# An FFT and two MLPs on one core: the second MLP's matmuls read their moving operand from the last column down, and its weight tiles lie at other addresses

## The chip, the cores and the metric

One Trainium2 chip, one core of it. The metric is the device time of the kernel in microseconds (us). Engines: PE is TensorE (PEld its weight loads, LDWEIGHTS), DVE is VectorE, ACT is ScalarE, POOL is GpSimd, SP is SyncE, which issues the DMAs that the text speaks of. SBUF is the on-chip memory of 128 partitions that the engines read; PSUM is where TensorE writes.

## What is computed

The reference is a chain of three parts, all in fp32:

```python
X = np.fft.fft(np.fft.fft(x, axis=1), axis=2).real      # x: 4 x 3072 x 256
h = X.reshape(-1, 256) @ w_in                           # first MLP, 256 -> 2048 -> 256
x = np.maximum(0.01 * h, h) @ w_out
xp = x shifted by one token within its sequence         # second MLP
xk = mu_k * x + (1 - mu_k) * xp
xr = mu_r * x + (1 - mu_r) * xp
k = np.maximum(xk @ w_k, 0)                             # 256 -> 1024
v = (k * k) @ w_v                                       # 1024 -> 256
out = sigmoid(xr @ w_r) * v                             # gate, 256 -> 256
```

Matrix products are made of float32r matmuls. Each operand is split into a high part of fewer bits and a low part that holds the rest, and a product is three matmuls: high by high, low weight by high data, high weight by low data.

## The kernel before, in words

**First part.** The FFT is folded by its symmetries and its second axis is merged into the weights of the first MLP, so the first part of the span alternates between FFT matmuls (L303), and, for each of 4 sequences, 3 tiles of tokens and 16 slices of the hidden width, the matmuls of the first MLP (L569, L581, L592). At four places per sequence L613 multiplies weights of only 2 columns (`dc[b]["w"]`, one column and its low part) with 512 moving columns. L387 builds the merged weights at the start, from plain f32 operands. Each of these results goes to DRAM tiles `yd` as 128 partitions (features) by tokens.

**Second MLP.** There are 24 tiles of 512 tokens (`tiles`, W = 512). A tile x is 128 partitions x 2 (halves of the 256 features) x 512 tokens. All its matmuls have a weight slice of 128 x 128 as the stationary operand and 512 token columns as the moving one.

- `load_tile` (L740, L745) loads x and the shifted x; `prep` (L748) mixes them on ACT and DVE (L751, L752) and splits the result into `mh` and `ml` (L104, L111).
- `k_mm` (L902, matmul on L908): for each of 8 slices f of the hidden width, 6 matmuls (3 products x 2 feature halves) into one PSUM tile.
- `k_ev` (L911 to L913): ACT takes the maximum with 0, DVE multiplies it with the PSUM tile to k squared, and `k_split` (L972) splits that into `k2h` and `k2l`.
- `v_mm` (L943, matmul on L951): for each slice f, 6 matmuls (3 products x 2 output halves) that add to two PSUM tiles over all 8 slices.
- `r_mm` (L953, matmul on L959): for each output half, 6 matmuls, then the sigmoid on ACT (L961) into `sig`.
- `finish` (L963): DVE multiplies `sig` with the sum of `v_mm` (L966), and SP issues the store of the tile. The last tile is stored in two halves.

So a tile has 48 + 48 + 12 matmuls. Each matmul has its own weight load in front of it. The order is written out by hand: in each step f the loop issues `k_mm`, the evaluation, the split of the slice before, a gate half in two of the eight steps, and then `drain`, which runs `v_mm` for a slice that was split a step or more earlier. `early` does two slices of the first tile between the last steps of the first MLP.

**Where the operands lie.** `w2_alloc` (L689) makes the pool `w2p` on the right side of SBUF while the first MLP of the last sequence runs: `wkh`, `wkl` (128 x 2 x 1024), `wvh`, `wvl` (128 x 8 x 256) and `wrh`, `wrl` (128 x 2 x 256), all float32r, one behind the other. Each is a multiple of 512 bytes in each partition. The parts of the first five pieces of the weights are computed early, kept in DRAM and loaded there by DMA; the other pieces, the gate's among them, are written straight into these tiles by ACT (high part, L161) and DVE (low part, L166). The moving tiles `mh`, `ml`, `k2h`, `k2l` lie in the pool `p2`, behind a pad of 64 bytes.

Of the kernel before, what the change touches and what calls it, by code (L numbers as in the profile page):

```python
# [9 lines left out]
F32 = mybir.dt.float32  # L10
F32R = mybir.dt.float32r
U32 = mybir.dt.uint32
ACTF = mybir.ActivationFunctionType
ALU = mybir.AluOpType
# [3 lines left out]
P = 128  # L18
# [3 lines left out]
D = 256  # L22
FF = 2048
FK = 1024
NF = FF // P
NK = FK // P
# [52 lines left out]
def fft_mlp_kernel(ctx, tc, xs, x7, x8, x87, tb, tbs, alt, ce, so, mu, w_in, w_out, w_k, w_v, w_r, out):  # L79
    nc = tc.nc  # L80
    ctx.enter_context(tc.manual_schedule())
    V, A, T, G, Q = nc.vector, nc.scalar, nc.tensor, nc.gpsimd, nc.sync
# [16 lines left out]
    pqp = tc.alloc_tile_pool(name="pqp", bufs=1)  # L99
    work = tc.alloc_tile_pool(name="work", bufs=1)  # L100
    fft = tc.alloc_tile_pool(name="fft", bufs=1, side="right")

    def act_copy(o, i):
        A.activation(o, i, ACTF.Copy)  # L104
# [572 lines left out]
    w2 = {}  # L677
# [3 lines left out]
    for q in range(4):  # L681
        sl, s2 = slice(q * 256, (q + 1) * 256), slice(2 * q, 2 * q + 2)
# [6 lines left out]
    def w2_alloc():  # L689
        w2p = tc.alloc_tile_pool(name="w2p", bufs=1, side="right")  # L690
        w2["pool"] = w2p
        for nm, k, f in (("k", 2, FK), ("v", NK, D), ("r", 2, D)):
            for x in "hl":
                w2[nm + x] = w2p.tile([P, k, f], F32R, name=f"w{nm}{x}")
        w2["xp"] = tc.alloc_tile_pool(name="xp", bufs=1, side="right")
        for n in range(n_early):
            nm, _, at = sources[n]
            for x, k in zip("hl", kept[n]):
                Q.dma_start(at(w2[nm + x]).bitcast(F32), k)
# [104 lines left out]
    for b in range(B):  # L804
# [4 lines left out]
        for ti in range(NT):  # L809
# [3 lines left out]
            for u in range(NF):  # L813
                i = ti * NF + u
                x = nx
# [40 lines left out]
                if b == B - 1 and i == qe_u + 2:  # L856
                    fft.release()
                    w2_alloc()
# [43 lines left out]
    def k_mm(ps, f, xk):  # L902
        hi, lo = xk
        sl = slice(f * P, (f + 1) * P)
        i = 0
        for w, x in ((w2["kh"], hi), (w2["kl"], hi), (w2["kh"], lo)):
            for k in range(2):
                T.matmul(ps, w[:, k, sl], x[:, k], start=(i == 0), stop=(i == 5))  # L908
                i += 1

    def k_ev(ps, r, k2):  # L911
# [7 lines left out]
    for f in range(2):  # L919
        early.append([ps_s.tile([P, 512], F32, tag="s", name="ps"), small("h"), small("f")])  # L920
        k_mm(early[f][0], f, ready[0]["k"])
        if f == 0:
            step(None, None)
        k_ev(*early[f])
# [18 lines left out]
    def v_mm(f, kk, vps):  # L943
        hi, lo = kk
        ws = ((w2["vh"], hi), (w2["vl"], hi), (w2["vh"], lo))
        order = [(i, m) for i in range(3) for m in range(NB)]
        if f == NK - 1:
            order = [(i, m) for m in range(NB) for i in range(3)]
        for i, m in order:
            w, x = ws[i]  # L950
            T.matmul(vps[m], w[:, f, m * P:(m + 1) * P], x, start=(f == 0 and i == 0), stop=(f == NK - 1 and i == 2))  # L951

    def r_mm(xr, sig, m):  # L953
        hi, lo = xr
        ps = ps2.tile([P, 512], F32, tag="rps", bufs=2, name="rps")
        i = 0
        for w, x in ((w2["rh"], hi), (w2["rl"], hi), (w2["rh"], lo)):
            for k in range(2):
                T.matmul(ps, w[:, k, m * P:(m + 1) * P], x[:, k], start=(i == 0), stop=(i == 5))  # L959
                i += 1  # L960
        A.activation(sig[:, m], ps, ACTF.Sigmoid)  # L961

    def finish(ti, vps, sig):  # L963
        o = p2.tile([P, NB, W], F32, tag="o", name="o")
        for m in range(NB):
            V.tensor_tensor(o[:, m], sig[:, m], vps[m], op=ALU.mult)  # L966
            if ti == len(tiles) - 1:
                Q.dma_start(out[ti, :, m], o[:, m])
        if ti < len(tiles) - 1:
            Q.dma_start(out[ti], o)  # L970
# [7 lines left out]
    def drain():  # L978
        if q2:
            t, f, kk = q2.pop(0)  # L980
            if f == 0:
                t["v"] = [ps2.tile([P, 512], F32, tag="v", bufs=4, name=f"v{m}") for m in range(NB)]
            v_mm(f, kk, t["v"])
            if f == NK - 1:
                finish(t["i"], t["v"], t["sig"])

    def gate(t, m):
        r_mm(t["rk"], t["sig"], m)

    q1, q2 = [], []  # L990
    for ti in range(len(tiles)):
# [7 lines left out]
        for f in range(f0, NK):  # L999
            ps = ps2.tile([P, 512], F32, tag="k", bufs=2, name="kps")  # L1000
            r = p2.tile([P, W], F32, tag="r", bufs=3, name="rl")
            k2 = p2.tile([P, W], F32, tag="k2", bufs=3, name="k2")
            k_mm(ps, f, rd["k"])
            k_ev(ps, r, k2)
            if q1:
                tt, ff, kk2 = q1.pop(0)
                q2.append((tt, ff, k_split(kk2)))
            q1.append((t, f, k2))
            t["rk"] = rd.get("r")
            if not end and g0 <= f < g0 + NB:  # L1010
                gate(t, f - g0)
            if end and f == NK - 1:
                gate(t, 0)
            if len(q2) > 1:
                drain()
            if f == f0:
                for n in ((1, 2) if ti == 0 else (ti + 2,)):
                    if n < len(tiles):
                        loaded[n] = load_tile(n)
            if f == f1 and not end:  # L1020
                for g in todo:
                    g()
                todo = do_prep(ti + 1)
            if todo:
                todo.pop(0)()
# [83 lines left out]
```

## Time and profile before

| | |
|---|---|
| time, median of 2 runs | 1493.05 us (1492.74 to 1493.37) |
| the profiled execution, first to last instruction | 1490.7 us |
| TensorE busy | 1472.8 us, 6524 matmuls |
| VectorE busy | 1029.6 us |
| ScalarE busy | 893.1 us |
| GpSimd busy | 150.2 us |
| mean granted TensorE clock | 0.998 |

The span of the profiled execution is 2.3 us under the median of the timed runs; what lies around the first and the last instruction is not in it. A row of the groups reads: line, engine, operation, out<-in by the program's names, partitions x elements and type, how many | busy time in us, mean ns of one | idle time before. A row of the timeline reads: start in us from the start of the span, time in us, engine, line, operation, operands, how many were merged into the row. Matmuls are pipelined: one starts before the end of the one before it, so the distance between two starts is shorter than a duration. In rows that merge n instructions the time runs from the first start to the last end.

### The profile page before, as it was taken

The page shows a single profiled execution, that of the slowest core. Times are in us where ns is not written, and L with a number is a line of the kernel's source. Part 1 is how long each engine was busy: PE and PEld are TensorE (multiplying, and loading weights), DVE is VectorE, ACT ScalarE, POOL GpSimd, SP SyncE. Part 2 cuts the span into 40 slices and gives each one's busy share as a digit, 9 for nine tenths or more (in the row PEclk, how much of TensorE's full clock was granted, in tenths as well). Part 3 has the DMA queues.
Part 4 walks back from the last instruction along what each step waited for, and adds up shares of the span by engine and source line. Part 5 has one row for each costly group of instructions (what it writes and reads, how often), then busy time and mean ns, then how long its engine had stood idle before and what let it go on. Part 6 is the DMA issues. An engine that isn't in the chain of part 4 may idle for free.

```text
span 1490.7 us, 17784 instructions
## 1 busy us (share of the span) xinstructions
PE 1472.8 (99%) x6524; PEld 1212.0 (81%) x6524; DVE 1029.6 (69%) x1436; ACT 893.1 (60%) x1475; POOL 150.2 (10%) x162
## 2 busy tenths in 40 slices
PE   7999999999999999999999999999999999999998
PEld 4788888888888888888888887888888888888887
DVE  7897667766667766666767665676767666666675
ACT  4666566656566565665666666556565655555554
POOL 2444201132010222010000000000000000000000
PEclk9999999999999999999999999999999999999999
DMA  8657323464132654141320102221212112221200
GB/s 319 164 181 163 54 82 125 167 123 91 17 106 91 199 115 79 36 155 64 108 79 0 57 1 92 78 85 43 85 48 80 60 68 63 65 71 57 72 29 29
DMA packets 86258, 134.23 MB, mean 90 GB/s; under 512 B 29158, under 2 KB 49383, under 8 KB 82586
## 3 DMA queue, kind: packets, MB, share of 16 engines
q1 hardware_dynamic: 70906, 86.49, 18.0%
q0 software_dynamic: 15264, 46.60, 12.6%
q8 instruction: 51, 0.84, 0.2%
q14 instruction: 37, 0.30, 0.1%
HBM read 105.19 MB, written 27.88 MB: 89 GB/s over the span
## 4 chain that ended last, share of the span: by engine, by line
PE 96%; DVE 2%; ACT 1%; DMA 0%; issue 0%; ACTq 0%; DVEq 0%
PE o L592 35%; PE v L951 17%; PE kps L908 17%; PE ps L581 9%; PE ps L569 9%; PE rps L959 4%; PE wps L387 1%; PE dps L613 1%; PE cps L436 0%; DVE fv L139 0%; DMA st<-in_w_in 0%; PE wps L389 0%; PE f1Qe L303 0%; PE f2Qe L303 0%; DVE t0Pe L287 0%; PE f0Qe L303 0%
## 5 line engine op out<-in xcount | busy, mean ns | idle before, releaser
L658 DVE SCALAR_TENSOR_TENSOR g<-ev,ps 128x512 f32<-128x512 f32 x192 | 131.7, 686 | 184.2 <-PE ps L581 183.9
L912 ACT ACTIVATE rl<-kps 128x512 f32<-128x512 f32 x190 | 113.8, 599 | 230.7 <-PE kps L908 227.2
L640 DVE TENSOR_TENSOR gl<-g,gh 128x1024 fp32r<-128x1024 f32 x192 | 239.3, 1246 | 1.4 <-ACT gh L104 1.4
L913 DVE SCALAR_TENSOR_TENSOR k<-kps,rl 128x512 f32<-128x512 f32 x190 | 131.6, 692 | 148.6 <-ACT rl L912 147.8
L104 ACT ACTIVATE gh<-g 128x1024 fp32r<-128x1024 f32 x192 | 202.9, 1057 | 51.9 <-PE o L592 50.9
L592 PE MATMUL o<-gh,uoh 128*128 128x512 f32 x768 | 211.8, 390 | 0.0
L592 PE MATMUL o<-gh,uol 128*128 128x512 f32 x768 | 211.1, 389 | 0.0
L592 PE MATMUL o<-gl,uoh 128*128 128x512 f32 x768 | 211.1, 389 | 0.0
L107 ACT ACTIVATE g<-ps 128x512 f32<-128x512 f32 x192 | 114.8, 598 | 156.2 <-DVE g L658 155.0
L592 PEld LDWEIGHTS o<-gh,uoh 128*128 128x128 f32 x768 | 144.7, 188 | 30.6
L592 PEld LDWEIGHTS o<-gh,uol 128*128 128x128 f32 x768 | 144.2, 188 | 30.0
L592 PEld LDWEIGHTS o<-gl,uoh 128*128 128x128 f32 x768 | 144.2, 188 | 29.9
L574 DVE SCALAR_TENSOR_TENSOR ev<-cb,w,ps 128x512 f32<-128x512 f32 x192 | 143.3, 746 | 2.3 <-DVE g L658 0.5
L111 DVE TENSOR_TENSOR k2l<-k,k2h 128x512 fp32r<-128x512 f32 x190 | 129.6, 682 | 0.5 <-ACT k2h L104 0.5
L951 PE MATMUL v<-k2h,wvh 128*128 128x512 f32 x382 | 121.6, 389 | 0.1
L951 PE MATMUL v<-k2l,wvh 128*128 128x512 f32 x382 | 121.5, 389 | 0.0
L951 PE MATMUL v<-k2h,wvl 128*128 128x512 f32 x382 | 121.5, 389 | 0.0
L107 ACT ACTIVATE g<-g 128x512 f32<-128x512 f32 x192 | 119.9, 624 | 0.0
L908 PE MATMUL kps<-mh,wkh 128*128 128x512 f32 x380 | 117.3, 390 | 1.5 <-ACT mh L104 0.8
L104 ACT ACTIVATE k2h<-k 128x512 fp32r<-128x512 f32 x190 | 118.4, 623 | 0.0
L908 PE MATMUL kps<-ml,wkh 128*128 128x512 f32 x380 | 117.2, 390 | 0.1
L908 PE MATMUL kps<-mh,wkl 128*128 128x512 f32 x380 | 117.0, 389 | 0.0
(407 smaller groups left out, 2257.1 us busy)
## 6 DMA issues: line engine op xcount, KB each, us to landing
y<-yo SPq DMA_DIRECT2D x24, 512.0 KB
xa<-y SPq DMA_DIRECT2D x24, 512.0 KB
out_dram<-o SPq DMA_DIRECT2D x23, 512.0 KB
tab_a<-in_tbs POOLq DMA_DIRECT2D x8, 1158.0 KB, 6.2
tab_b<-in_tbs POOLq DMA_DIRECT2D x8, 1158.0 KB, 5.4
tab_c<-in_tbs POOLq DMA_DIRECT2D x6, 1158.0 KB, 5.4
tab_d<-in_tbs POOLq DMA_DIRECT2D x6, 1158.0 KB, 5.8
pm<-in_xs POOLq DMA_DIRECT2D x54, 128.0 KB, 3.4
```

The costliest lines, as they stand in the source:

```text
L104: A.activation(o, i, ACTF.Copy)
L107: A.activation(o, i, ACTF.Prelu, alpha=0.01)
L111: V.tensor_tensor(lo, src, hi.bitcast(F32), op=ALU.subtract)
L569: T.matmul(x["ps"], l[:, f], r, start=(i == 0), stop=(i == 2))
L574: V.scalar_tensor_tensor(x["ev"], x["cb"], w128[:, u:u + 1], x["ps"], op0=ALU.mult, op1=ALU.add)
L581: T.matmul(x["ps"], l[:, f], r, start=False, stop=(i == 2), skip_group_check=True)
L592: T.matmul(po[s][h], w[:, u % HF, h * P:(h + 1) * P], g[:, s], start=(u == 0 and i == 0), stop=(u == NF - 1 and i == 2))
L640: V.tensor_tensor(gl, x["g"], x["gh"].bitcast(F32), op=ALU.subtract)
L658: V.scalar_tensor_tensor(g[:, 1], x["ev"], 2.0, x["ps"], op0=ALU.mult, op1=ALU.subtract)
L908: T.matmul(ps, w[:, k, sl], x[:, k], start=(i == 0), stop=(i == 5))
L913: V.scalar_tensor_tensor(k2, ps, 0.0, r, op0=ALU.max, op1=ALU.mult)
L951: T.matmul(vps[m], w[:, f, m * P:(m + 1) * P], x, start=(f == 0 and i == 0), stop=(f == NK - 1 and i == 2))
```

## The change

All matmuls of the second MLP read their moving operand with a step of -1, from column 511 down to column 0. The product of `k_mm` therefore comes out with its tokens reversed, `v_mm` reverses it again, and the gate, which also comes out reversed, is read reversed in `finish`. The gate's high and low weights share one tile with the two parts in turn, so that a part's columns are 8 bytes apart. Behind the four other weight tiles lie pads of 128, 128, 128 and 384 bytes, so that the tiles start at four places modulo 512 bytes.

```diff
+    def back(w):
+        return w[:, ::-1]
...
         w2["pool"] = w2p
-        for nm, k, f in (("k", 2, FK), ("v", NK, D), ("r", 2, D)):
+        for nm, k, f in (("k", 2, FK), ("v", NK, D)):
             for x in "hl":
                 w2[nm + x] = w2p.tile([P, k, f], F32R, name=f"w{nm}{x}")
+                w2p.tile([P, 96 if nm + x == "vl" else 32], F32, name=f"pad{nm}{x}")
+        wr = w2p.tile([P, 2, D, 2], F32R, name="wr")
+        w2["rh"], w2["rl"] = wr[:, :, :, 0], wr[:, :, :, 1]
...
-                T.matmul(ps, w[:, k, sl], x[:, k], start=(i == 0), stop=(i == 5))
+                T.matmul(ps, w[:, k, sl], back(x[:, k]), start=(i == 0), stop=(i == 5))
...
-            T.matmul(vps[m], w[:, f, m * P:(m + 1) * P], x, start=(f == 0 and i == 0), stop=(f == NK - 1 and i == 2))
+            T.matmul(vps[m], w[:, f, m * P:(m + 1) * P], back(x), start=(f == 0 and i == 0), stop=(f == NK - 1 and i == 2))
...
-                T.matmul(ps, w[:, k, m * P:(m + 1) * P], x[:, k], start=(i == 0), stop=(i == 5))
+                T.matmul(ps, w[:, k, m * P:(m + 1) * P], back(x[:, k]), start=(i == 0), stop=(i == 5))
...
-            V.tensor_tensor(o[:, m], sig[:, m], vps[m], op=ALU.mult)
+            V.tensor_tensor(o[:, m], back(sig[:, m]), vps[m], op=ALU.mult)
```

The first edit of a matmul is in `k_mm` (L908), the second in `v_mm` (L951), the third in `r_mm` (L959).

## Rows read from the trace of the kernel before

**Rows 1.** The page: span, TensorE's share, granted clock in 40 slices

```profile
span 1490.7 us, 17784 instructions
PE 1472.8 (99%) x6524; PEld 1212.0 (81%) x6524; DVE 1029.6 (69%) x1436; ACT 893.1 (60%) x1475; POOL 150.2 (10%) x162
PEclk9999999999999999999999999999999999999999
```

**Rows 2.** The page: the chain that ended last, by engine and by line

```profile
PE 96%; DVE 2%; ACT 1%; DMA 0%; issue 0%; ACTq 0%; DVEq 0%
PE o L592 35%; PE v L951 17%; PE kps L908 17%; PE ps L581 9%; PE ps L569 9%; PE rps L959 4%; PE wps L387 1%; PE dps L613 1%; PE cps L436 0%; DVE fv L139 0%; DMA st<-in_w_in 0%; PE wps L389 0%; PE f1Qe L303 0%; PE f2Qe L303 0%; DVE t0Pe L287 0%; PE f0Qe L303 0%
```

**Rows 3.** Busy time by stretch: the second MLP from 925 us

```profile
core 0: us, PE busy (x) PEld busy (x) DVE busy (x) ACT busy (x) POOL busy (x), PEclk, DMA share, GB/s
925.00:1484.10 559.10, 559.10 (x2468) 462.94 (x2468) 380.26 (x552) 328.99 (x546) 0.00 (x0) 1.00 0.19 62
```

**Rows 4.** Groups of instructions by line and form: the second MLP's matmuls

```profile
L951 PE MATMUL v<-k2h,wvh 128*128 128x512 f32 x382 | 121.6, 389 | 0.1
...
L908 PE MATMUL kps<-mh,wkh 128*128 128x512 f32 x380 | 117.3, 390 | 1.5 <-ACT mh L104 0.8 <-ACT yo L104 0.7
...
L959 PE MATMUL rps<-mh,wrh 128*128 128x512 f32 x96 | 29.6, 389 | 0.0
...
L908 PE MATMUL ps<-mh,wkh 128*128 128x512 f32 x4 | 1.3, 396 | 0.0
...
L951 PE MATMUL v<-er,wvh 128*128 128x512 f32 x4 | 1.3, 395 | 0.0
...
L951 PE MATMUL v<-er,wvl 128*128 128x512 f32 x2 | 0.6, 398 | 0.0
```

**Rows 5.** Timeline of PE and PEld, second MLP, around 1121 us

```profile
1120.90 0.39 PE L951 MATMUL v<-k2h,wvh 128*128 128x512 f32 x1
1120.91 0.19 PEld L951 LDWEIGHTS v<-k2h,wvl 128*128 128x128 f32 x1
1121.13 0.39 PE L951 MATMUL v<-k2h,wvl 128*128 128x512 f32 x1
...
1122.04 0.39 PE L951 MATMUL v<-k2l,wvh 128*128 128x512 f32 x1
...
1122.26 0.61 PE L908 MATMUL kps<-mh,wkh 128*128 128x512 f32 x2
```

**Rows 6.** Timeline of PE, 39 to 41 us, and the clock of that stretch

```profile
39.24 0.63 PE L581 MATMUL ps<-Ql,wh 128*128 128x512 f32 x1
39.66 0.63 PE L581 MATMUL ps<-Qh,wl 128*128 128x512 f32 x1
40.09 0.63 PE L569 MATMUL ps<-Ph,wh 128*128 128x512 f32 x1
40.52 0.63 PE L569 MATMUL ps<-Pl,wh 128*128 128x512 f32 x1
...
39.20:41.40 2.20, 2.20 (x7) 1.68 (x6) 1.79 (x4) 2.17 (x5) 1.80 (x1) 0.50 0.72 194
```

**Rows 7.** Tile wps: count, duration ns minimum/median/maximum of its f32 matmuls

```profile
L387 PE MATMUL wps<-fv,cet x32: 377/379/792, 6.6 to 98.4; 128*128 128x256 f32 x32
...
L387 PE MATMUL wps<-fv,sot x32: 377/378/634, 9.2 to 99.5; 128*128 128x256 f32 x32
```

**Rows 8.** Timeline of PE, second MLP, 905 to 911 us

```profile
905.61 0.63 PE L908 MATMUL kps<-mh,wkh 128*128 128x512 f32 x2
...
909.79 0.63 PE L959 MATMUL rps<-mh,wrh 128*128 128x512 f32 x2
```

**Rows 9.** Timeline of PE around L613, and its loads' durations beside the gate's

```profile
119.04 1.07 PE L592 MATMUL o<-gl,uoh 128*128 128x512 f32 x4
119.94 0.40 PE L613 MATMUL dps<-wh,dcs 128*2 128x512 f32 x1
120.18 0.40 PE L613 MATMUL dps<-wl,dcs 128*2 128x512 f32 x1
120.41 0.39 PE L581 MATMUL ps<-Qh,wh 128*128 128x512 f32 x1
...
121.80 1.07 PE L592 MATMUL o<-gh,uoh 128*128 128x512 f32 x4
122.71 0.39 PE L592 MATMUL o<-gh,uol 128*128 128x512 f32 x1
...
L613 PEld LDWEIGHTS dps<-wh,dcs x16: 82/83/83, 119.7 to 768.0; 128*2 128x2 f32 x16
...
L959 PEld LDWEIGHTS rps<-mh,wrh x96: 187/188/188, 909.6 to 1482.7; 128*128 128x128 f32 x96
```

**Rows 10.** DVE's last product: its group from 900 us, and the timeline's end

```profile
L966 DVE TENSOR_TENSOR o<-sig,v 128x512 f32<-128x512 f32 x48 | 30.8, 681 | 3.0 <-PE v L951 2.9
...
1486.26 1.44 DVE L966 TENSOR_TENSOR o<-sig,v 128x512 f32<-128x512 f32 x2 [2.92 <-PE v L951]
```

**Rows 11.** Tile wrh: the writing of the gate's weights

```profile
L161 ACT ACTIVATE wrh<-fv x1: 615/615/615, 841.0 to 841.0; 128x512 fp32r<-128x512 f32 x1
L166 DVE SCALAR_TENSOR_TENSOR wrl<-r,wrh x1: 686/686/686, 849.6 to 849.6; 128x512 fp32r<-128x512 f32 x1
```

## The prediction

> **What bounds the kernel now.** I read the page's engine shares first: TensorE is busy for 1472.8 of 1490.7 us, at the granted clock's upper level in every slice [rows 1]. The chain that ended last says the same, 96% PE, and its L951, L908 and L959 are the three matmul lines of the second MLP, which the change edits [rows 2]. Then the stretch by itself: from 925 to 1484.1 us PE is busy for all of 559.10 us at clock 1.00, while DVE is busy for 380.26 us and ACT for 328.99 us [rows 3]. So the other engines have a third of that stretch free, no DMA ends a wait of PE there, and the time of the stretch is the number of matmuls times the distance from one start to the next.
>
> The number: L908 has 3 × 380 + 3 × 4 = 1152 matmuls, L951 3 × 382 + 4 + 2 = 1152, L959 3 × 96 = 288, together 2592 (one row of each kind stands in [rows 4]; the forms left out have the same counts). All stream 512 columns.
>
> The distance: in the timeline the six matmuls from 1120.90 to 1122.26 take 1.36 us, 226.7 ns each, and the next four kinds keep that [rows 5]. 512 columns at 2.4 GHz are 213.3 ns, so each matmul carries 13.3 ns of excess, 2592 × 13.3 = 34.5 us in all. This is the most that any edit of operand addresses can win here, since no instruction goes.
>
> Where does the excess come from? Three places of the trace speak to it.
> First, at the lower clock level (clock 0.50) the same f32r matmuls start at 39.24, 39.66, 40.09 and 40.52, 427 ns apart, which is 512 columns at 1.2 GHz with no excess [rows 6]. So it is a cost of streaming at full rate.
> Second, the plain f32 matmuls of L387 last 377 to 379 ns [rows 7]; a matmul of the second MLP lasts 389 and is followed after 226.7, so duration less 162 is the distance, and L387 runs at 215 to 217 ns. That is the lowest distance that any wide matmul shows here, with a weight load before each.
> Third, the excess is not a constant of the shape: the same lines between 905.61 and 909.79 take 4.18 us for 18 matmuls, 232.2 ns each [rows 8], before they settle at 226.7. So timing or addresses do enter, by some 6 ns.
>
> **The change, part by part.**
>
> *Places of the weight tiles, interleaved gate weights.* These act through the weight load, which reads while the matmul before it streams. The trace has a test of that: L613 loads weights of 2 columns, 83 ns against 188 for 128 columns. The four L592 matmuls from 119.04 to 119.94, the last of which streams beside such a short load, take 0.90 us, 225 ns each, and the two L613 themselves, the first of which also streams beside a short load, take 0.47 us, 235 ns each [rows 9]. Take away 126 of 128 weight columns and the stream gets shorter by 2 ns at most (the rounding of the view is as large), or even longer. So where weights lie should be worth about nothing: bounds 0 to -2 ns × 2592 = -5 us; I take 0.
> The Trainium skill speaks against this half too ("SBUF — State Buffer", section "Who interferes with whom"): TensorE reads moving data and weights through two ports that are independent of each other. L613 agrees with it; by that rule these edits are worth exactly 0.
>
> *Moving operands from the last column down.* The number of columns, matmuls and weight loads stays, and no row of this trace has a descending read. Bounds by the nearest rows: below, the f32 distance of 216 ns, that is (226.7 - 216) × 2592 = 27.7 us won; above, the same lines not settled, (232.2 - 226.7) × 2592 = 14.3 us lost, and L613's 235 ns, 21.5 us lost [rows 9]. Far beyond these lies a read that gets only every second cycle: 427 ns, 519 us lost, by the distance of [rows 6]. The row nearest to the changed matmul is its own, same shape, type and clock, 226.7 ns. I take 0.
> The Trainium skill has a rule by which more would be possible ("TensorE: Matmul & The Clock Gate", section "Wait — 56ns, not 53.3ns?"): matmuls back to back start 215.7 ns apart at 512 columns. The rows of the second MLP disagree with it by 11.0 ns each; by the rule the sum would be 28.5 us less. I treat it as a rival below, priced from the f32 rows.
>
> *Reversed gate in the last product.* The gate comes out reversed, so L966 reads one operand from its end: 48 instructions of 681 ns [rows 10]. If a descending read took twice the time, that would be 33 us more on DVE, spread over a stretch in which it has 179 us free; only the last pair, 1.44 us at the very end, is on the path [rows 10]. Bounds 0 to +1.4 us, taken as 0. If DVE had no room there, PE would wait for PSUM; by the busy share it has.
>
> *Writing the interleaved gate weights.* One ACT instruction of 615 ns and one DVE instruction of 686 ns, at 841 and 849.6 us [rows 11], write every second word. Twice their time is 1.3 us once, while PE works on the first MLP; 0. The pads are tiles that nothing reads or writes. No DMA, wait or queue is moved.
>
> The sum: 1490.7 us of span, plus 2.3 us that lie around it in the median of the runs (1493.05), plus 0: **1493.0 us**, no change.
>
> **The rivals.**
>
> *The excess goes.* If the excess is a collision between the order in which the two reads sweep the memory, a common direction and chosen places could end it: 216 ns, 27.7 us less, **1465 us**. If it goes in part, anything between. For it: the excess is there only at full rate, absent in f32 with the same weight loads, and varies with timing [rows 6 to 8]. Against it: the short weight loads did not lower it [rows 9]. To reach a gain of 2% (29.9 us) all 2592 matmuls would have to come to 215.2 ns, under the median of both f32 rows [rows 7]; even the full success of this case lies just short of that.
>
> *The settled state is lost.* The lines settle at 226.7 only after 925 us, and after L613 the seven matmuls from 120.18 to 121.80 take 1.62 us, 231 ns each, before L592 is at 0.91 us for four [rows 8, 9]. If the descending reads or the mixed places never settle, the second MLP stays at the 232.2 ns of [rows 8] for all of its length: +14.3 us, **1507 us**; with 235 ns +21.5 us, 1514. It decides from the first microseconds after 900 and shows in any ten matmuls thereafter.
>
> *The gate's strided weights load slower.* A load costs (188 - 83) / 126 = 0.83 ns for a column [rows 9]. Should words 8 bytes apart come at half that rate, L959's loads take 188 + 107 = 295 ns, and since a matmul starts some 35 ns after its load (1120.91 + 0.19 to 1121.13 in [rows 5]), the distance in the gate becomes 330 ns: 288 × 103 = 29.7 us more, **1523 us**. It counts from the point where a load exceeds some 190 to 220 ns. Against it: a load runs at one column per 0.83 ns, less than half the rate of the moving read, so it has the more time for each.
>
> *Descending reads at half rate.* 519 us more, **2012 us**. Nothing in the trace speaks for it or against it.
>
> **How the numbers follow.** No change (1491 to 1496): 0.42. The excess goes, wholly or in part (1463 to 1487): 0.32. Settled state lost (1500 to 1514): 0.16. Strided loads (1503 to 1525): 0.05. Half rate: 0.05. The range from 1463 to 1512 leaves out half rate, most of the strided loads and the ends of the others, some 0.15. 2% (29.9 us) is about what a measurement of this kernel can tell from no change. Faster by more than that needs the far end of the first rival: 0.08. Slower by more is half rate, half of the strided loads and a little for two losses together: 0.09. Within 2%: 0.83. Where a change of either sign holds so much of the chance, the likeliest case's own range is 1491 to 1496.
>
> **What would show it.** Right: the starts of L908, L951 and L959 after 930 us stay 226 to 227 ns apart, their durations 389 ns, the gate's loads 188 ns, and PE's busy time stays within 2 us. Wrong: matmul durations near 378 ns (the excess was a matter of order or place, and my reading of L613 failed), durations of 393 to 401 after 930 us (not settled), loads of L959 over 220 ns, or L951 at twice its time. If only L959's distance changes, the interleaving did it; if all three lines change alike, the direction or the places did.

## The result, and the profile after

The changed kernel takes 1507.75 us (1507.72 to 1507.78, two runs) against 1493.05 before: ratio 1.0099, interval 1.007 to 1.0129. It is 14.7 us slower. The forecast was no change.

The page after, span, busy times and granted clock:

```profile
span 1506.0 us, 17784 instructions
...
PE 1487.8 (99%) x6524; PEld 1213.8 (81%) x6524; DVE 1029.3 (68%) x1436; ACT 892.7 (59%) x1475; POOL 148.9 (10%) x162
...
PEclk9999999999999999999999999999999999999999
```

Against [rows 1] PE is busy 15.0 us longer with the same 6524 matmuls, the span is 15.3 us longer, and DVE, ACT and POOL have moved by no more than 1.3 us. So each matmul takes longer, not more of them and not a wait.

The same stretch as [rows 3], in the same columns:

```profile
925.00:1484.10 559.10, 559.10 (x2398) 452.86 (x2397) 372.49 (x540) 321.11 (x534) 0.00 (x0) 1.00 0.19 62
```

In 559.10 us, all of them busy, it starts 2398 matmuls instead of 2468: 233.2 ns each instead of 226.5. A window also counts what is running when it opens, so these means lie 0.1 to 0.2 ns under the settled distances, which are 233.3 and 226.7. Some 2480 matmuls of the second MLP start after 925 us; at 6.67 ns each that is 16.5 us. The 120 or so ahead of 925 us were slow before too [rows 8].

The span is longer by only 15.3 us, as the first part, which the change doesn't touch, came out 1.4 us shorter. The first matmul of `k_mm` behind the end of the first MLP, before and after, and the busy times of two earlier stretches, before and after (columns as in [rows 3]):

```profile
899.56 0.73 PE L908 MATMUL kps<-mh,wkh 128*128 128x512 f32 x2 [0.69 <-ACT yo L104]
...
898.17 0.73 PE L914 MATMUL kps<-mh,wkh 128*128 128x512 f32 x2 [0.69 <-ACT yo L107]
```

```profile
20.00:60.00 40.00, 35.31 (x144) 25.14 (x144) 33.21 (x61) 24.98 (x45) 17.92 (x14) 0.96 0.82 246
...
20.00:60.00 40.00, 35.36 (x153) 25.09 (x152) 34.07 (x62) 24.84 (x45) 18.40 (x15) 1.00 0.82 247
39.20:41.40 2.20, 2.20 (x12) 1.79 (x11) 1.81 (x4) 2.09 (x4) 1.76 (x1) 1.00 0.74 198
```

Near 40 us the trace before fell to the lower clock level, 0.50, and started 7 matmuls in 2.2 us [rows 6]; the trace after stayed at 1.00 and started 12. In the 9 us ahead of 39 us PE had been busy for 4.92 us before and 4.96 us after. From these `k_mm` matmuls to the end of the span it is 591.2 us before and 607.8 after: the second MLP takes 16.7 us longer, and the 14.7 us of the medians hide some 2 of them.

The groups by line and form, columns as in [rows 4]; the first line is the first MLP, which was not edited:

```profile
L595 PE MATMUL o<-gh,uoh 128*128 128x512 f32 x768 | 211.3, 389 | 0.0
...
L957 PE MATMUL v<-k2h,wvh 128*128 128x512 f32 x382 | 124.5, 398 | 0.0
...
L914 PE MATMUL kps<-mh,wkh 128*128 128x512 f32 x380 | 120.1, 398 | 1.5 <-ACT mh L107 0.8 <-ACT yo L107 0.7
```

The timeline at the place of [rows 5] (PE alone, two matmuls merged in a row):

```profile
1119.82 0.63 PE L957 MATMUL v<-k2h,wvh 128*128 128x512 f32 x2
1120.29 0.63 PE L957 MATMUL v<-k2h,wvl 128*128 128x512 f32 x2
...
1122.62 0.63 PE L957 MATMUL v<-k2h,wvh 128*128 128x512 f32 x2
```

Twelve matmuls in 2.80 us, 233.3 ns each, where [rows 5] has 226.7. The duration went from 389 to 397 ns and the distance from 226.7 to 233.3, so duration less 162 to 164 still gives the distance. All three lines changed alike and without scatter: the matmuls are not unsettled, they are settled at another value.

The tile of the gate's PSUM result (duration in ns: least / median / most, first and last start, form), and the last product's instructions by source line, after:

```profile
L965 PEld LDWEIGHTS rps<-mh,wr x192: 195/197/197, 908.2 to 1498.3; 128*128 128x128 f32 x192
L965 PE MATMUL rps<-mh,wr x192: 397/397/404, 908.4 to 1498.5; 128*128 128x512 f32 x192
```

```profile
L972 DVE TENSOR_TENSOR o<-sig,v x48: 679/681/686, 925.9 to 1502.3; 128x512 f32<-128x512 f32 x48
```

The interleaved weights load in 197 ns instead of 188, and the product that reads the gate from its end takes the 681 ns of [rows 10].

### The profile page after: what moved, and what is told of

Same layout as the page of the kernel before. It is cut to its first block, busy times and chain, and to the rows that moved or that the text cites. A ratio compares the mean times of both kernels' runs of the same rounds, so it can differ in the third digit from the quotient of the medians.

```text
span 1506.0 us, 17784 instructions
## 1 busy us (share of the span) xinstructions
PE 1487.8 (99%) x6524; PEld 1213.8 (81%) x6524; DVE 1029.3 (68%) x1436; ACT 892.7 (59%) x1475; POOL 148.9 (10%) x162
## 3 DMA queue, kind: packets, MB, share of 16 engines
q1 hardware_dynamic: 70906, 86.49, 17.8%
## 4 chain that ended last, share of the span: by engine, by line
PE 96%; DVE 2%; ACT 1%; DMA 0%; issue 0%; POOL 0%; POOLq 0%; DVEq 0%; ACTq 0%
PE o L595 34%; PE v L957 18%; PE kps L914 18%; PE ps L584 9%; PE ps L572 8%; PE rps L965 4%; PE wps L390 1%; PE dps L616 0%; PE cps L439 0%; DVE fv L142 0%; DMA st<-in_w_in 0%; PE f1Qe L306 0%; PE f2Qe L306 0%; DVE t0Pe L290 0%; PE f0Qe L306 0%
## 5 line engine op out<-in xcount | busy, mean ns | idle before, releaser
L110 ACT ACTIVATE g<-ps 128x512 f32<-128x512 f32 x192 | 114.7, 598 | 156.8 <-DVE g L661 155.5
L110 ACT ACTIVATE g<-g 128x512 f32<-128x512 f32 x192 | 119.8, 624 | 0.0
```

Of the source, the lines that this page charges most:

```text
L110: A.activation(o, i, ACTF.Prelu, alpha=0.01)
```

## The experiments

A distance below is that of two starts, taken in the settled part. In the three kernels that are tables, each line of the program is one stretch of 112 or 224 matmuls that go round four PSUM banks; a row shows one bank, so from its first to its last start there are 27 × 4 = 108 distances (or 55 × 4 = 220).

### The direction alone

The changed kernel with the weight tiles where they were before; only `back()` stays, in the three matmuls and the last product.

```diff
-                w2p.tile([P, 96 if nm + x == "vl" else 32], F32, name=f"pad{nm}{x}")
-        wr = w2p.tile([P, 2, D, 2], F32R, name="wr")
+        for nm, k, f in (("k", 2, FK), ("v", NK, D), ("r", 2, D)):
```

> Only the descending moving reads (and the reversed gate in the last product); all weight tiles back at their old places, gate parts apart. Theory D, the direction alone lengthens each stream from 226.7 to 233.3 ns: about 1507.7 us, matmuls of the second MLP at 397 ns. Theory P, the places alone do it: 1493 us, 389 ns. Theory DP, only both together do it: 1493 us here and in the next run as well.

Measured: 1508.53 us (1507.75 to 1509.6), ratio 1.0111 (1.0096 to 1.0126). The busy times of a stretch, and the tile of `v_mm`'s result:

```profile
930.00:1450.00 520.00, 520.00 (x2231) 418.95 (x2230) 344.97 (x500) 299.44 (x497) 0.00 (x0) 1.00 0.20 64
```

```profile
L954 PE MATMUL v<-k2h,wvl x382: 395/397/398, 903.5 to 1501.8; 128*128 128x512 f32 x191
```

2231 matmuls in 520 us are 233.1 ns each, and the durations are those of the whole change. From the first of those `k_mm` matmuls to the end of the span it is 607.8 us, as with the whole change. The direction by itself costs all of it.

### The places alone

The kernel before with the four pads, read upward, the gate's parts in two tiles as before.

```diff
                 w2[nm + x] = w2p.tile([P, k, f], F32R, name=f"w{nm}{x}")
+                if nm != "r":
+                    w2p.tile([P, 96 if nm + x == "vl" else 32], F32, name=f"pad{nm}{x}")
```

> Only the pads behind the four weight tiles, moving operands read upward, gate parts apart. Theory D: 1493 us, 389 ns. Theory P: about 1507 us, 395 to 398 ns. Theory DP: 1493 us.

Measured: 1507.69 us (1507.01 to 1507.85), ratio 1.0104 (1.0089 to 1.0119). The busy times of the same stretch, and the tiles of `v_mm`'s and the gate's results:

```profile
930.00:1450.00 520.00, 520.00 (x2238) 420.29 (x2237) 346.72 (x503) 301.38 (x499) 0.00 (x0) 1.00 0.20 64
```

```profile
L953 PE MATMUL v<-k2h,wvl x382: 389/397/404, 905.4 to 1501.5; 128*128 128x512 f32 x191
```

```profile
L961 PE MATMUL rps<-mh,wrh x96: 387/393/397, 910.4 to 1498.0; 128*128 128x512 f32 x96
```

Nearly the same loss in sum, but another picture: durations spread from 387 to 404 ns, distances from 224 to 241, to the last tile; 520 us / 2238 is a mean of 232.4 ns. The second MLP takes 605.7 us here, 14.6 more than before. So the places alone cost nearly all of it too, and the two together cost no more than the direction does. The prediction had put them at nothing.

### The gate's interleaving alone

```diff
+        wr = w2p.tile([P, 2, D, 2], F32R, name="wr")
+        w2["rh"], w2["rl"] = wr[..., 0], wr[..., 1]
```

> Only the gate's two weight parts interleaved in one tile; no pads, moving operands read upward. Under D and P the interleaving costs at most what the gate's own 288 matmuls can: 288 x 6.7 ns = 1.9 us, so 1493 to 1495 us, and nothing at all in the k and v products. If the strided loads upset the settled distance of their neighbours too: up to 1507 us.

Measured: 1495.11 us (1494.37 to 1495.8), ratio 1.002 (1.0011 to 1.003). The tile of the gate's result:

```profile
L961 PEld LDWEIGHTS rps<-mh,wr x192: 193/193/194, 910.7 to 1486.4; 128*128 128x128 f32 x192
L961 PE MATMUL rps<-mh,wr x192: 392/394/398, 911.0 to 1486.6; 128*128 128x512 f32 x192
```

The gate's 288 matmuls go to 233.3 ns apart, 288 × 6.6 = 1.9 us, while `v_mm` and `k_mm` stay within 0.2 ns of 226.7. Of the 2.75 us against the kernel before on the same chip (1492.36), 2.1 lie in the second MLP by the trace. With the direction reversed this price is already paid.

### A table of places and directions

The computation is replaced by stretches like `for i in range(112): T.matmul(banks[i % 4], w[:, 32:160], x[:, 0:512][:, ::-1], start=True, stop=True)`, each with other weight columns or another direction. A weight column is 4 bytes; `x` and `w` start at the same place modulo 512 bytes.

> Leaves out the whole computation: one moving tile and one weight tile, 68 stretches of 112 matmuls (two of 224) with different place of the weights against the moving tile (bytes 0 to 504), both directions, weight step 1 or 2, 128, 32 or 2 weight columns. Theory D: every stretch upward at 389 ns and every one downward at 397, wherever the weights lie. Theory P: 389 ns only where both lie at the same place modulo 512, up to 400 elsewhere, in both directions. Theory L, the excess comes from the load's reads meeting the stream's: 2 weight columns give 375 to 380 ns in both directions; if instead L is false they stay at 389 or more.

The rows of six stretches, one PSUM bank each (L94 weights at 0 bytes upward; L95 the same downward; L106 weights at 128 bytes upward; L110 at 256 bytes upward; L111 the same downward; L144 weights of 2 columns at 0 bytes upward):

```profile
L94 PE MATMUL ba<-x,w x28: 389/389/792, 6.4 to 33.9; 128*128 128x512 f32 x28
...
L95 PE MATMUL ba<-x,w x28: 397/397/398, 34.8 to 60.0; 128*128 128x512 f32 x28
...
L106 PE MATMUL ba<-x,w x28: 390/393/404, 322.1 to 347.2; 128*128 128x512 f32 x28
...
L110 PE MATMUL ba<-x,w x28: 389/389/397, 426.0 to 450.5; 128*128 128x512 f32 x28
...
L111 PE MATMUL ba<-x,w x28: 397/397/398, 451.5 to 476.7; 128*128 128x512 f32 x28
...
L144 PE MATMUL ba<-x,w x28: 396/396/402, 1310.9 to 1336.0; 128*2 128x512 f32 x28
```

L95: (60.0 - 34.8) / 108 = 233.3 ns. L110: 24.5 / 108 = 226.9. L106: 25.1 / 108 = 232.4. The settled distances of the whole table:

```
weights' place - moving operand's, modulo 512 bytes   upward, ns   downward, ns
0                                                     226.7        233.3
8                                                     230.7        233.3
16, 32, 64                                            233.3        233.3
96                                                    234.3        233.3
128                                                   232.3        233.3
192                                                   228.9        233.3
256                                                   226.7        233.3
320                                                   233.3        233.3
384                                                   232.3        233.3
448                                                   228.9        233.3
480, 504                                              233.3        233.3
0, weights 2 or 32 columns wide (loads 83, 108 ns)    231.7        233.3
256, weights 2 columns wide                           228.9        233.3
0, weight columns 8 bytes apart (loads 193 ns)        233.3        233.3
places mixed as in the changed kernel                 232.4        233.3
```

Three things follow. Downward is 233.3 ns in every one of the stretches, whatever the weights do. Upward the distance depends on where the weights lie: 226.7 is what it takes when they lie at the same place as the moving operand modulo 256 bytes (modulo 512 isn't needed), and every other place of the table costs 2 to 8 ns. And a load of 2 columns, or of 32, at the right place does not shorten the stream: it lengthens it by 5 ns. With both operands shifted by 512 bytes and the weights then at +0 or +256, and with both shifted by 64 or 128 bytes, it is 226.7 or 226.8 again, so the difference of the places counts; the next table shows where that ends. No other engine works in these stretches, so neither its reads nor its transfers cause the differences.

### Places 256 bytes apart

If the place modulo 256 is what counts, pads of 256 bytes must cost nothing.

```diff
-                    w2p.tile([P, 96 if nm + x == "vl" else 32], F32, name=f"pad{nm}{x}")
+                    w2p.tile([P, 64], F32, name=f"pad{nm}{x}")
```

> The kernel before with pads of 256 bytes behind the four k and v weight tiles, so that the tiles lie at the moving operands' place or 256 bytes from it, upward reads, gate parts apart. Theory P256 (the table's: only the distance modulo 256 bytes counts): 1493 us, matmuls at 389 ns. Theory P512 (any tile off the place modulo 512 costs, or several places at once cost): about 1500 to 1507 us.

Measured: 1492.6 us (1490.91 to 1493.46), ratio 0.9998 (0.9988 to 1.0008). The tile of `v_mm`'s result:

```profile
L953 PE MATMUL v<-k2h,wvl x382: 387/389/398, 904.8 to 1486.4; 128*128 128x512 f32 x191
```

All of the loss of the places is gone, in the kernel itself.

### Two tables of the order of reading

Two more kernels of stretches, in which the moving operand is read in other orders. The products are written to PSUM one behind the other, but for five stretches of the second of these kernels, which put them back in natural order.

> Leaves out the whole computation: 67 stretches of 112 matmuls on one moving and one weight tile. Columns of the moving operand 128 to 512, weights 16 to 128 columns, places 4 to 272 bytes, moving columns permuted (blocks in descending order, steps 2, 4, 16, 256), one PSUM bank, and bf16 operands. Theory R (the excess is a slower read of 4-byte columns, in proportion to them): distance = columns x 0.456 ns downward and x 0.443 upward, so 58 and 57 ns at 128 columns; bf16 at 216 ns in both directions; blocks in descending order that are read upward inside cost no more than upward. Theory C (a fixed cost for each matmul): 20 ns above columns / 2.4 downward at every count, so 73 ns at 128; bf16 as f32r. Under both, one PSUM bank changes nothing.

Rows of five stretches (L136: two blocks of 256 columns, the upper first, upward inside; L138: 32 blocks of 16, the same way; L140: every second column, then the others; L143: columns 0, 256, 1, 257 and so on; L162: bf16 upward):

```profile
L136 PE MATMUL ba<-x,w x28: 389/389/396, 893.2 to 917.7; 128*128 128x512 f32 x28
...
L138 PE MATMUL ba<-x,w x28: 395/397/398, 944.0 to 969.2; 128*128 128x512 f32 x28
...
L140 PE MATMUL ba<-x,w x28: 616/632/632, 996.3 to 1045.0; 128*128 128x512 f32 x28
...
L143 PE MATMUL ba<-x,w x28: 379/379/396, 1147.0 to 1170.3; 128*128 128x512 f32 x28
...
L162 PE MATMUL bb<-xb,wb x28: 379/379/379, 1780.8 to 1804.1; 128*128 128x512 bf16 x28
```

With the weights at 0 or 256 bytes, blocks of 256 or 64 columns taken downward cost nothing (226.7 ns), and blocks of 16, 4 or 1 cost the whole 6.6. Bf16 has 2.4 ns left of the excess over 213.3: 23.3 / 108 = 215.7 ns, in both directions and at both places tried. One PSUM bank instead of four changes nothing (226.7 and 233.3).

Both theories of the width fell. Over columns / 2.4, the excess upward is 13.3 ns at 256, 384 and 512 columns and some 16 to 17 at 448, 480 and 504, so it isn't in proportion to the columns; downward it is 11.7 ns at 256, 17.8 at 384 and 20 at 512, so there it isn't fixed either. At 128 columns both directions take 111.7 ns, more than either theory had.

The table also limits what was said of the places. Rows of two stretches in which both operands are shifted alike and read upward (L128 by 4 bytes, L132 by 16):

```profile
L128 PE MATMUL ba<-x,w x28: 392/400/401, 684.2 to 709.9; 128*128 128x512 f32 x28
...
L132 PE MATMUL ba<-x,w x28: 393/393/395, 789.6 to 814.6; 128*128 128x512 f32 x28
```

The difference of the places is 0 in both, and yet they settle at 237.8 and 231.1 ns (8 bytes: 231.1); shifted by 32 bytes it is 226.7 again. So the place itself counts too, below 32 bytes. Downward such shifts cost as well: 236.7 ns at 4 bytes, 235.6 at 8.

And L143 shows something new: float32r columns read by turns from the two halves start 215.8 ns apart, as bf16 does, and do so at weight places 0, 128 and 256 bytes.

> Leaves out the whole computation: 30 stretches of 112 matmuls with moving columns taken by turns from several places of one row: single columns from 2, 4, 8 or 16 equal parts, runs of 2 to 64 from the two halves, halves at other distances, and for the runs also with the output put back in natural order. Theory A (columns taken by turns from two places have more time for each place's next fetch): single columns and short runs from two parts at 216 ns (379 ns duration), the same at every place of the weights; runs of 16 or 64 back at 226 to 233. Theory K (only a distance of 1024 bytes between neighbours helps): other distances and four or more parts at 226 to 460. The output in natural order: 216 as well if writing pairs of columns costs nothing, above 400 if it does.

Rows of three stretches (L98: by turns from two halves; L99: from four quarters; L102: by turns from two halves, two columns at a time):

```profile
L98 PE MATMUL ba<-x,w x28: 378/379/379, 34.3 to 57.6; 128*128 128x512 f32 x28
...
L99 PE MATMUL ba<-x,w x28: 433/451/451, 58.5 to 89.0; 128*128 128x512 f32 x28
...
L102 PE MATMUL ba<-x,w x28: 507/507/523, 193.4 to 228.9; 128*128 128x512 f32 x28
```

Two halves, single columns: 215.8 ns, also with the second half 260 to 512 columns (1040 to 2048 bytes) behind the first. Four parts 283, eight 487, sixteen 435; two columns at a time 328, four 250, sixteen 240; every second column of each half first (0, 256, 2, 258 and so on) 226.7. For the runs, natural order in the output changes nothing. So one order is fast and its neighbours are slow: theory A fell for short runs, and theory K's distance of 1024 bytes isn't needed. By what mechanism of the memory the two halves are fast was not found.

### By turns, in the second MLP

```diff
+    def turns(w):
+        return w.rearrange("p (a b) -> p b a", a=2)
+    def packed(ps):
+        return ps.rearrange("p (b a) -> p b a", a=2)
...
-                T.matmul(ps, w[:, k, sl], x[:, k], start=(i == 0), stop=(i == 5))
+                T.matmul(packed(ps), w[:, k, sl], turns(x[:, k]), start=(i == 0), stop=(i == 5))
```

The same edit in `v_mm` and `r_mm`, at the old places; the product at the end puts the tokens back in order with views of its three operands.

> The kernel before, with every moving operand of the second MLP read by turns from its two halves (columns 0, 256, 1, 257, ...), all weight tiles at their old places; the last product puts the tokens back in order. If the table's 215.8 ns hold in the kernel (A): 2592 x (226.7 - 215.8) = 28.1 us less, 1464 to 1465 us, matmuls of the second MLP at 379 ns. If other engines' reads beside it, or the accumulation into PSUM, spoil it (S): 389 ns or more and 1493 us or above.

Measured: 1464.37 us (1462.82 to 1465.26), ratio 0.9812 (0.9798 to 0.9827). A stretch, the tile of `v_mm`'s result, and the last product by its line:

```profile
930.00:1450.00 520.00, 520.00 (x2411) 455.36 (x2410) 374.84 (x539) 320.54 (x534) 0.00 (x0) 1.00 0.20 66
```

```profile
L957 PE MATMUL v<-k2h,wvl x382: 379/379/379, 904.4 to 1458.3; 128*128 128x512 f32 x191
```

```profile
L972 DVE TENSOR_TENSOR o<-sig,v x48: 686/841/846, 926.0 to 1459.0; 128x512 f32<-128x512 f32 x48
```

520 us / 2411 = 215.7 ns; the settled distance is 215.8. 2592 times the 10.84 ns between 226.67 and 215.83 is 28.1 us, and the kernel before, beside it, took 1492.31: 27.9 us won. Theory A held. The product takes 841 ns instead of 681, which DVE's free time hides but for the last pair.

### By turns, in both MLPs

The same for the first MLP's matmuls (three lines), with `turns` and `packed` in the instruction that joins their PSUM tile with `cb`, and the order put back where the result is copied out.

> As the run before, and the 3456 matmuls of the first MLP the same way, with the broadcast row and the store of its result read in permuted order. A: 3456 x 10.8 = 37.5 us less again, about 1427 us. If VectorE or ScalarE pay for the permuted reads and end the waits in the first part (V): between 1430 and 1480 us, with PE waiting for L574's group or for the copies to yo.

Measured: 1430.53 us (1429.29 to 1431.38), ratio 0.9588 (0.9572 to 0.9604): faster than both kernels of this study. Two groups by form, from the lists of PE and of DVE:

```profile
L598 PE MATMUL o<-gh,uoh 128*128 128x512 f32 x768 | 203.0, 379 | 0.0
...
L580 DVE SCALAR_TENSOR_TENSOR ev<-cb,w,ps 128x512 f32<-128x512 f32 x192 | 145.9, 760 | 2.1 <-DVE g L664 0.5
```

3456 matmuls at 10.84 ns are 37.5 us; PE's busy time fell by 37.3 from the run above (1444.5 to 1407.2), the span by 34.8 (1462.8 to 1428.0). The 2.5 us between are idle time of PE that the faster stream opened; 1.4 of them are waits of PE for L580. So the stream gained what theory A has, and a little of theory V came with it. L580 pays 14 ns for its order of reading (746 ns before).

### Why the first tile was slow before

[rows 8] were read as matmuls that had not settled yet. By the table they could as well be matmuls whose moving operand lies elsewhere. This kernel is the one before with 96 bytes behind the weight tiles and 160 more in front of the later tiles' operands, so that all have the place modulo 256 of the first tile's operands.

```diff
+        w2p.tile([P, 24], F32, name="padw")
...
-    p2.tile([P, 16], F32, tag="pad", bufs=1, name="pad3")
+    p2.tile([P, 56], F32, tag="pad", bufs=1, name="pad3")
```

> The kernel before with every weight tile of the second MLP and every moving tile of its pool moved by a pad, by the same distance modulo 256 bytes, so that both also agree with the place of the first tile's operands, which lie in another pool. Theory P256: the matmuls between 900 and 925 us, which took 232 ns, take 226.7 from the start, 0.6 us in all, and the rest stays at 389 ns, as the place itself does not count, only the distance between the two. Theory T (settling is a matter of time after the stall at 900 us): still 232 ns there. Theory F (the place itself counts): other than 389 ns throughout, 1500 us or more.

Measured: 1492.24 us, one run, the kernel before beside it 1493.09. The tile of `v_mm`'s result, its six matmuls on the first tile, and the timeline of PE in the stretch of [rows 8]:

```profile
L952 PE MATMUL v<-er,wvh x4: 389/389/389, 901.0 to 902.1; 128*128 128x512 f32 x4
...
L952 PE MATMUL v<-er,wvl x2: 389/389/389, 901.4 to 901.7; 128*128 128x512 f32 x2
```

```profile
905.51 0.62 PE L909 MATMUL kps<-mh,wkh 128*128 128x512 f32 x2
905.96 0.61 PE L909 MATMUL kps<-mh,wkl 128*128 128x512 f32 x2
...
909.59 0.62 PE L960 MATMUL rps<-mh,wrh 128*128 128x512 f32 x2
```

18 matmuls in 4.08 us, 226.7 ns, where [rows 8] have 4.18 us and 232.2; the six `er` matmuls last 389 ns where [rows 4] have 395 and 398. So the first tile was slow by the place of its operands. The gate's and some of `v_mm`'s operands of that tile lie in `p2` already and were slow as well, in turn with `k_mm`'s; they too come to 226.7 when only the places change. Time has a small part: after each wait of PE near 900, 904 and 910 us some five matmuls still run at 228 to 236 ns, and after the one at 919 us some ten at 224 to 240.

## Why the prediction was wrong

**What bounds the kernel: right.** PE is the bound, the number of matmuls and loads is unchanged, and the whole difference lies in the distance between starts, as the prediction's first part had it. Its reading that the excess over 213.3 ns belongs to streaming at the full rate held for float32r: bf16 has 2.4 of the 13.3 ns, and what float32r takes beyond bf16 was there to be won, 27.9 us in the second MLP against the 27.7 that the prediction gave as its bound. That these agree is in part luck: the 216 ns of that bound come from plain f32 matmuls of 256 columns [rows 7], another type and another width. One reading was wrong, without effect on the forecast: the clock was not at the upper level throughout the trace before, as [rows 6] show.

**Places of the weight tiles: the first step that failed.** "So where weights lie should be worth about nothing: bounds 0 to -2 ns" came from [rows 9], where a load of 2 columns did not shorten the stream. The table shows that a short load can't stand for a load that is out of the way: beside loads of 2 to 112 columns the stream settles at 228.9 to 231.7 ns. Of the weights measured beside an upward stream, only 128 columns at the moving operand's place modulo 256 bytes (or one column ahead of it: 226.7 at 252 bytes too) leave it at 226.7. What made L613 itself slow, the short load or the places of its own operands, no run separates. The places alone cost 15.3 us (1507.69 against 1492.36 for the kernel before on the same chip). The Trainium skill ("SBUF — State Buffer", section "Who interferes with whom") gives TensorE two independent ports for moving data and weights; that the place of one changes the time of the other by up to 8 ns in 227 disagrees with reading this as no effect, and the measurement decides.

**Moving operands from the last column down: the second step that failed.** "The row nearest to the changed matmul is its own, same shape, type and clock, 226.7 ns. I take 0." The runs put in its place 233.3 ns, 397 ns of duration, at every place of the weights. The upper bound that the prediction drew from [rows 8], 14.3 us, is near the 16.7 us that the second MLP lost, but the row meant something else: there it was the place of the first tile's operands, as the last experiment shows, here it is the direction. So the rival "the settled state is lost" has about the size and not the mechanism: after the change the settled matmuls don't scatter, they sit at 397. That its time, 1507 us, was met so closely is in part luck, as the medians hide some 2 us of the loss.

**The two together.** The prediction took the terms as a sum. They aren't: direction 233.1, places 232.4, both 233.2. With a downward read the places of these tiles cost nothing more.

**The excess goes: the rival that was half right.** It took the excess for a collision of two sweeps that "a common direction and chosen places could end". Places end 6.6 of the 20 ns over 213.3, and none of those tried gets below 226.7; the reversed direction adds. What ends the rest is an order of reading that the change doesn't have. For the best orders the Trainium skill's 215.7 ns ("TensorE: Matmul & The Clock Gate", section "Wait — 56ns, not 53.3ns?") agrees with the runs, 215.8 for bf16 and for float32r by turns, and disagrees with float32r read in order.

**The small terms: right but for one.** The reversed gate in the last product costs nothing (681 ns in [rows 10] and after). The interleaved weights load in 193 to 197 ns, not in 295, so the rival of strided loads falls (its counter, "less than half the rate of the moving read", is a little off: 0.83 ns against 226.7 / 512 = 0.44 is just over half); alone they cost the gate's own 1.9 us, which the prediction had at 0.

## What to carry to other kernels

Where PE is busy without a gap, the distance between starts is worth measuring to the nanosecond, and a stretch that runs slower than another of the same shape is worth an explanation by its addresses before one by time. For float32r with 512 columns, lay each 128-column weight slice at the moving operand's place modulo 256 bytes, both at multiples of 32 bytes, and read upward; or read the moving operand by turns from its two halves, where the three places of the weights that were tried made no difference and 10.8 of the 13.3 ns of excess go. A row that takes work away (a short load) tests the amount of that work only, and not where it lies.

## What the hardware showed that was not expected

- A float32r matmul of 512 columns at the full clock settles at 215.8 ns (two halves by turns), 226.7 (upward, places equal modulo 256 bytes and at multiples of 32) or 233.3 (downward, at multiples of 16); nearly all other places, upward, lie between 228 and 238. The plain f32 matmuls of 256 columns in [rows 7] start as far apart as the first of these.
- Downward costs by the width: nothing at 128 and 256 columns (111.7 both ways; 120.0 up, 118.4 down), 2 to 4.5 ns at 384 to 504, 6.6 at 512.
- It costs by the block too, with 512 columns: 226.7 ns with blocks of 64 columns, 233.3 with blocks of 16.
- Every second column takes 451 ns, every fourth 461, every sixteenth 433, but a step of 256 takes 215.8.
- A load whose columns are 8 bytes apart takes 193 ns, and 197 beside a downward read, against 188.
- What causes these distances is open: the runs show where they occur, and none shows the mechanism.
